# RWKV-6 attention feeding a squared-ReLU MLP: the order of the opening written anew

## The chip, the cores and the metric

The kernel runs on one core of one Trainium2 chip. The metric is device time in microseconds (us), the median of a few runs; lower is better. A core has five instruction queues that run beside each other and meet only at semaphores: PE (matrix products), DVE (vector engine), ACT (scalar engine), POOL (GpSimd) and SP, which here issues every DMA. Each engine takes its instructions strictly in program order, so an instruction that waits holds up all that stands behind it on the same engine.

## The reference

```python
for t in range(S):                       # r, k, v, w: (4, 8, 768, 48); u: (8, 48)
    cur = np.einsum('bhd,bhe->bhde', u[None] * kt, vt)
    y[:, :, t] = np.einsum('bhd,bhde->bhe', rt, state + cur)
    state = wt[:, :, :, None] * state + np.einsum('bhd,bhe->bhde', kt, vt)
...
h = x @ w_in                             # x: y as (3072, 384); w_in (384, 2048)
r = np.maximum(h, 0.0)
return ((r * r) @ w_out)                 # w_out (2048, 384)
```

A linear attention with a per-channel decay `w` and a bonus `u` for the current token, then a two-layer MLP (the names of the code call it MoE) on all 3072 tokens.

## The kernel before

**Tiles.** The 768 tokens of each of 4 batches are cut into 3 blocks of 256, so there are 12 steps, 0 to 11. In a step a partition holds two neighbouring tokens, and 64 partitions form a chunk. For each step the attention part makes a 256 x 384 block `y`; the MLP part multiplies it with `w_in` (8 groups of 256 columns) and `w_out` (4 groups of 512 rows for each half of the tokens).

**An order written by hand.** The text `ORDER` is the whole program. Each word names an operation, its step and further indices, after a colon the PSUM bank that it writes, after `=` the engine (A is ACT, V is DVE, G is POOL). The loop at the end of the kernel reads the words and calls one Python function for each; each engine's instruction order is the order of its words in the text. There is no planner.

**The words of a step s**, with the line by which the profile knows them:

- `ld.s.w/r/k/v` load 384 KB each (L201); `ld.0.u` loads the 1.5 KB of `u` into one partition (L229); `ld.g.i` and `ld.g.o` load 768 KB of `w_in` and `w_out` (L209, L214), and `cast.i.g`, `cast.o.g` turn them to fp16 (L221). All loads go through SP's one queue.
- `ub_` spreads `u` over the partitions by a product (L234), `uc_` copies it out of PSUM (L238).
- `ww_` multiplies neighbouring decays (L288), `lw_` takes the logarithm (L292), `cum_` makes prefix sums by products (L332 to L336), `exp_` and `ac_` take exponentials (L349, L356).
- `rw_` and `kw_` scale r and k by w (L300, L304); `rd_.s.0` and `rd_.s.1` apply the decays to r and k (L370); `tr_` transposes them on PE (L379) and `rkt_` copies the transposes to SBUF (L384).
- `p_` makes the r times k products (L404), two for a step, `pm_` masks them (L412 where they lie in two single banks, L415 in a double bank).
- `v_` casts v (L296); `su_` makes the state update (L426), `ts_` adds the old state (L434, L436), `sn_` decays the sum on POOL (L440).
- `ku_`, `qp_` on POOL, `q_` on DVE and `vq_` on POOL make the bonus term (L307, L312, L315, L318).
- `y_`, `yc_`, `yq_` add the three parts of y in one double bank (L450), `ysb_` copies it out (L488), `yt_` transposes it (L496), `xt_` copies that (L500).
- `m1_.s.g` are the six products of group g with `w_in` (L513); groups 2c and 2c+1 need `cast.i.c`. `rl_.s.g` applies ReLU (L520 on ACT, L522 on DVE), `sq_` squares (L528), `m2_.s.c.q` multiplies with `w_out` (L536), `os_` and `store` write out.
- `warm_.n.i` are n products of zeros of 512 columns into bank i (L618); their result is not used.

PSUM holds two double banks `att` (0 and 1) and four single banks `one` (0 to 3): a word that writes a bank waits until the last reader of its former contents is done.

The call that turns a word into instructions:

```python
for word in ORDER.split():
    ...
    operations[name](*args)
```

Of the kernel before, what the change touches and what calls it, by code (L numbers as in the profile page):

```python
# [14 lines left out]


ORDER = """
ld.0.w warm_.10.1 ld.1.w ld.0.u ld.0.r ld.0.k ld.1.k ww_.0=V lw_.0 ld.1.r cum_.0:1 ww_.1=V ub_:1 lw_.1 exp_.0 ld.0.v
rw_.0=G ac_.0 warm_.1.3 uc_=A cum_.1:0 ld.0.i kw_.0=V warm_.4.3 ku_.0 ac_.1 rd_.0.0 exp_.1 ld.1.v rd_.0.1 tr_.0.0:0
rkt_.0.0=A kw_.1=V ld.1.i tr_.0.1:1 rw_.1=G rd_.1.1 warm_.4.2 ld.2.i rkt_.0.1=A ld.3.i qp_.0 warm_.1.0 rd_.1.0 v_.0=A  # L20
ld.2.w p_.0.0:n pm_.0.0 su_.0:1 tr_.1.1:2 ts_.0.0=A q_.0 p_.0.1:0 rkt_.1.1=A sn_.0.0 warm_.4.0 pm_.0.1 ld.2.k
cast.i.0=A vq_.0 tr_.1.0:3 rkt_.1.0=V y_.0:0 v_.1=A ku_.1 ts_.0.1=V yc_.0 yq_.0 ld.2.r p_.1.1:n ysb_.0=A p_.1.0:1
pm_.1.1 cast.i.1=A yt_.0:3 sn_.0.1 su_.1:0 xt_.0=V qp_.1 ts_.1.0=V m1_.0.1:3 cast.i.2=A pm_.1.0 m1_.0.3:2 m1_.0.0:0
rl_.0.1=A sn_.1.0 q_.1 ld.2.v cast.i.3=A m1_.0.2:1 rl_.0.3=V m1_.0.4:3 vq_.1 ld.0.o ts_.1.1=V rl_.0.2=A y_.1:1
rl_.0.0=V yc_.1 ld.3.k ww_.2=G yq_.1 m1_.0.5:2 ysb_.1=V ku_.2 m1_.0.6:0 lw_.2 rl_.0.4=V rl_.0.5=A yt_.1:1 sq_.0.0=A
cum_.2:1 ld.1.o xt_.1=V m1_.0.7:3 ld.3.w kw_.2=G rl_.0.6=A m1_.1.1:1 ld.2.o exp_.2 sn_.1.1 m1_.1.4:2 rl_.1.1=V
rl_.0.7=A m1_.1.0:0 rw_.2=G sq_.0.3=A rl_.1.4=V m1_.1.5:1 rl_.1.0=V qp_.2 m1_.1.7:2 rd_.2.0 rl_.1.5=A m1_.1.6:0 ld.3.r
rl_.1.7=A rd_.2.1 tr_.2.0:3 cast.o.0=G rl_.1.6=A m1_.1.2:1 ld.3.o rkt_.2.0=V v_.2=A tr_.2.1:2 rl_.1.2=A m1_.1.3:0
ku_.3 rkt_.2.1=V ac_.2 sq_.1.0=A su_.2:0 q_.2 m2_.0.0.0:1 ld.4.w m2_.0.1.0:3 ts_.2.0=V sq_.0.1=A cast.o.1=G rl_.1.3=V
ld.3.v p_.2.0:1 p_.2.1:0 ww_.3=V sq_.1.1=A m2_.1.1.0:0 vq_.2 m2_.1.0.0:2 pm_.2.1 lw_.3 sq_.1.2=A m2_.0.0.1 pm_.2.0  # L30
m2_.1.1.1 sn_.2.0 sq_.1.3=A m2_.1.0.1 cast.o.2=A m2_.0.1.1 ld.4.k qp_.3 cum_.3:0 y_.2:1 sq_.0.2=A yc_.2 yq_.2 ld.4.r
q_.3 m2_.1.1.2 cast.o.3=A m2_.1.0.2 rw_.3=V ld.5.w ww_.4=G m2_.0.0.2 ysb_.2=V ac_.3 exp_.3 m2_.0.0.3 kw_.3=G ld.4.v
m2_.1.1.3 rd_.3.0 os_.0.0=A lw_.4 v_.3=G m2_.1.0.3 ld.5.r rd_.3.1 os_.1.1=A yt_.2:1 kw_.4=G cum_.4:1 os_.1.0=V xt_.2=A
tr_.3.0:0 ac_.4 su_.3:0 exp_.4 tr_.3.1:2 ld.5.v ts_.3.0=V rw_.4=G m2_.0.1.2 rkt_.3.0=V rkt_.3.1=A m1_.2.0:1 sn_.3.0
ld.6.w rd_.4.0 m2_.0.1.3 ww_.5=G ts_.3.1=V m1_.2.6:2 ld.5.k os_.0.1=A rd_.4.1 v_.4=G m1_.2.3:0 ld.7.w ku_.4 p_.3.1:1
rl_.2.3=A p_.3.0:0 pm_.3.1 m1_.2.1:3 lw_.5 rl_.2.0=A store.0.0 m1_.2.2:0 rl_.2.1=A dtr_.4.1 pm_.3.0 vq_.3 m1_.2.5:1
sq_.2.0=A su_.4:1 rl_.2.6=V rl_.2.5=A y_.3:0 qp_.4 rl_.2.2=V yc_.3 yq_.3 m1_.2.7:3 ysb_.3=A dtr_.4.0 m1_.2.4:1
sq_.2.1=A rl_.2.7=V sn_.3.1 cum_.5:0 v_.5=G yt_.3:2 ts_.4.0=V ac_.5 m2_.2.0.0:0 rl_.2.4=V xt_.3=A kw_.5=G m2_.2.0.1
q_.4 sq_.2.2=A m2_.2.1.0:2 sn_.4.0 rw_.5=V exp_.5 m2_.2.1.1 ku_.5 m2_.2.1.2 sq_.2.3=A rd_.5.0 m1_.3.7:1 rd_.5.1
dtr_.5.0 m1_.3.1:3 qp_.5 ts_.4.1=V m2_.2.1.3 rl_.3.1=A rl_.3.7=V dtr_.5.1 p_.4.1:0 p_.4.0:1 os_.2.1=V m1_.3.3:1  # L40
pm_.4.0 vq_.4 store.1.1 m2_.2.0.2 ld.6.r rl_.3.3=A pm_.4.1 m1_.3.2:2 ld.6.k sn_.4.1 m1_.3.0:3 ld.7.r rl_.3.2=A ww_.6=G
ld.7.k sq_.3.1=A su_.5:1 y_.4:0 ts_.5.0=V ww_.7=G yc_.4 q_.5 yq_.4 store.1.0 p_.5.0:1 ysb_.4=A m1_.3.5:2 ld.6.v
rl_.3.0=V lw_.7 m2_.2.0.3 pm_.5.0 yt_.4:1 os_.2.0=A m1_.3.4:3 ld.8.w xt_.4=V lw_.6 ku_.6 rl_.3.5=V p_.5.1:1 rl_.3.4=A
cum_.7:0 pm_.5.1 ld.8.r m1_.3.6:0 exp_.7 vq_.5 m1_.4.3:1 sq_.3.0=A rw_.7=V ld.7.v cum_.6:1 m1_.4.1:3 rl_.4.3=A kw_.7=G
m1_.4.0:2 rl_.4.1=A store.2.1 m1_.4.5:1 rl_.3.6=A rl_.4.0=V sn_.5.0 exp_.6 m2_.3.1.0:3 rd_.7.0 kw_.6=G sq_.3.2=A
m2_.3.0.0:0 rd_.7.1 m2_.3.0.1 rw_.6=G rl_.4.5=A m2_.3.1.1 sq_.3.3=A ww_.8=G rd_.6.0 m2_.3.0.2 ac_.7 m1_.4.4:1 qp_.6
rd_.6.1 dtr_.6.0 m2_.3.0.3 ac_.6 m1_.4.2:2 v_.6=A dtr_.6.1 ku_.7 q_.6 v_.7=A su_.6:1 y_.5:0 ld.11.w os_.3.0=V yc_.5
ld.9.w rl_.4.4=V vq_.6 yq_.5 ld.8.k m2_.3.1.2 rl_.4.2=V ysb_.5=A m2_.3.1.3 rw_.8=V ts_.6.0=A store.3.0 yt_.5:1 sn_.6.0
ld.8.v os_.3.1=A m1_.4.7:0 xt_.5=A qp_.7 m1_.4.6:3 ts_.6.1=V sq_.4.2=A m1_.5.7:2 rl_.4.6=A p_.6.1:1 rl_.5.7=V
store.0.1 p_.6.0:0 rl_.4.7=A sn_.6.1 m1_.5.0:1 pm_.6.1 lw_.8 m1_.5.1:3 sq_.4.0=A ld.9.k ww_.9=G pm_.6.0 m1_.5.5:0  # L50
rl_.5.1=A m1_.5.4:2 dtr_.7.0 sq_.4.3=A rl_.5.0=V y_.6:1 sq_.4.1=V rl_.5.5=A su_.7:0 yc_.6 rl_.5.4=A kw_.8=V yq_.6 q_.7
m2_.4.0.0:3 ysb_.6=A m1_.5.6:2 v_.8=A ts_.7.0=V dyt_.6 vq_.7 cum_.8:1 rl_.5.6=A m2_.4.1.0:0 ni_.8=V sq_.5.0=A dtr_.7.1
m2_.4.0.1 tw_.1=V sn_.7.0 m2_.4.0.2 ac_.8 exp_.8 store.3.1 m2_.4.0.3 ww_.11=V ld.9.r lw_.9 m1_.5.3:1 ku_.8 os_.4.0=A
ld.10.w rd_.8.1 m2_.4.1.1 sq_.5.2=A ld.9.v m2_.4.1.2 ts_.7.1=V rl_.5.3=A tw_.3=V m1_.5.2:3 dtr_.8.1 qp_.8 m1_.6.3:2
# [621 lines left out]
```

## Time and profile before

| | |
|---|---|
| runs of the kernel, us | 179.25, 179.38, 216.63; median 179.38 |
| the profiled execution | 178.85 us, of which 177.0 from its first to its last instruction |
| PE busy | 169.8 us, 96% of the span |
| DVE, ACT, POOL busy | 144.5, 136.9, 129.6 us |
| mean granted TensorE clock | 0.998 |
| bytes moved | 35.63 MB |

The profiled execution lies 0.53 us below the median. Times inside a profile count from the start of its span. A row of the timeline gives start, duration, engine, line, operation, output<-input with shapes, how many instructions were merged, and in square brackets how long the engine had been idle before and what ended that. `SPq` rows are issues of DMAs on SP's queue.

### The profile page before, as it was taken

The numbers are of one execution on the slowest core, as the hardware profiler recorded it, in microseconds if no ns is written. First come the engines' busy times: TensorE is split into PE (matmuls) and PEld (weight loads), VectorE is DVE, ScalarE is ACT, GpSimd is POOL, SyncE is SP. The second block draws the span as 40 slices with busy tenths as digits, with TensorE's granted clock in tenths as the row PEclk, the third lists the DMA queues.
The fourth block names the chain that finished last, engine by engine and source line by source line (L and its number), as shares of the span: only waits on it lengthen the run. The fifth ranks groups of instructions, "written<-read, shape, count | busy, mean of one in ns | idle before, by whom it ended". The sixth has DMA issues, their size and how long they took to land.

```text
span 177.0 us, 5877 instructions
## 1 busy us (share of the span) xinstructions
PE 169.8 (96%) x2458; PEld 135.5 (77%) x2458; DVE 144.5 (82%) x228; ACT 136.9 (77%) x225; POOL 129.6 (73%) x117
## 2 busy tenths in 40 slices
PE   7978899999999999999999999999999999999992
PEld 2355789756777687767867889888888888999992
DVE  6499967956787889768989999899999999559960
ACT  5779798998868756987998898999898855893301
POOL 6389999996699994989759709935996871282760
PEclk9999999999999999999999999999999999999999
DMA  5999999999999299989999979969969100410223
GB/s 156 325 357 390 354 231 368 355 351 249 299 254 204 47 219 323 275 194 211 311 137 209 280 63 242 211 95 278 198 152 163 45 3 4 133 48 0 87 95 133
DMA packets 78811, 35.63 MB, mean 201 GB/s; under 512 B 72129, under 2 KB 77250, under 8 KB 78786
## 3 DMA queue, kind: packets, MB, share of 16 engines
q1 hardware_dynamic: 78786, 35.27, 78.8%
q8 instruction: 19, 0.31, 0.7%
q14 instruction: 6, 0.05, 0.1%
HBM read 25.17 MB, written 4.72 MB: 169 GB/s over the span
## 4 chain that ended last, share of the span: by engine, by line
PE 73%; DVE 9%; DMA 7%; SPq 6%; issue 2%; POOL 1%; ACT 1%; ACTq 0%; DVEq 0%; POOLq 0%
PE one L513 29%; PE one L590 15%; PE one L536 15%; PE att L450 6%; DMA w_st_b<-in_moe_w_in_dram 5%; SPq L201 3%; DVE pmT_b L415 3%; PE att L404 3%; DMA r_b<-in_r_dram 2%; PE att L426 2%; DVE w_st_b L568 2%; SPq L209 1%; PE one L379 1%; DVE rdec_buf L370 1%; DVE q_b L315 1%
## 5 line engine op out<-in xcount | busy, mean ns | idle before, releaser
L513 PE MATMUL one<-xT_b,wi_sb 128*128 128x256 bf16 x576 | 70.8, 273 | 0.7 <-ACT gt_b L520 0.3
L513 PEld LDWEIGHTS <-wi_sb 128*128 128x128 f16 x576 | 54.9, 98 | 9.6 <-issue 1.5
L520 ACT ACTIVATE gt_b<-one 128x512 f16<-128x512 f32 x65 | 37.8, 596 | 12.1 <-PE one L513 11.2
L528 ACT ACTIVATE gt_b<-gt_b 128x1024 bf16<-128x1024 f16 x44 | 45.8, 1054 | 0.6 <-DVE gt_b L522 0.2
L536 PE MATMUL one<-wo_sb,gt_b 128*128 128x384 f16 x160 | 28.7, 326 | 0.0
L415 DVE TENSOR_TENSOR pmT_b<-att,mask 128x1024 bf16<-128x1024 f32 x22 | 26.2, 1214 | 1.3 <-PE att L404 1.3
L522 DVE TENSOR_SCALAR gt_b<-one 128x512 f16<-128x512 f32 x31 | 20.9, 685 | 5.4 <-PE one L513 4.4
L307 POOL TENSOR_TENSOR ku_b<-k_b,u_bc 128x768 f32<-128x768 f32 x12 | 22.4, 1869 | 3.0 <-DMA k_b<-in_k_dram 2.3
L440 POOL TENSOR_TENSOR S_b<-t_b,ac_buf 128x384 bf16<-128x384 f32 x20 | 18.1, 906 | 8.9 <-DVE t_b L436 4.5
L590 PEld LDWEIGHTS <-gt_b 128*128 128x128 bf16 x280 | 23.4, 98 | 0.6 <-issue 0.2
L312 POOL TENSOR_TENSOR ku_b<-ku_b,r_b 128x768 f32<-128x768 f32 x12 | 22.4, 1863 | 0.6 <-DMA r_b<-in_r_dram 0.4
L536 PEld LDWEIGHTS <-gt_b 128*128 128x128 bf16 x160 | 15.2, 98 | 9.2 <-issue 0.2
L318 POOL TENSOR_TENSOR vq_b<-v_b,q_b 128x768 bf16<-128x768 f32 x12 | 18.5, 1539 | 4.1 <-PE att L450 3.0
L590 PE MATMUL one<-wo_sb,gt_b 128*128 128x192 f16 x168 | 17.0, 246 | 0.0
L315 DVE TENSOR_REDUCE q_b<-ku_b 128x16 f32<-128x768 f32 x12 | 11.3, 945 | 3.7 <-POOL ku_b L312 3.7
L370 DVE TENSOR_TENSOR rdec_buf<-r_b,att 128x768 bf16<-128x768 f32 x12 | 11.4, 948 | 2.3 <-ACT att L349 1.8
L595 ACT ACTIVATE w_st_b<-one 128x192 f32<-128x192 f32 x13 | 4.3, 330 | 10.9 <-PE one L590 10.9
L300 POOL TENSOR_TENSOR r_b<-r_b,w_b 128x384 f32<-128x384 f32 x8 | 8.0, 1001 | 5.1 <-DMA r_b<-in_r_dram 5.1
L370 DVE TENSOR_TENSOR rdec_buf<-k_b,att 128x768 bf16<-128x768 f32 x12 | 11.4, 946 | 0.1
L568 POOL TENSOR_TENSOR gt_b<-gt_b 128x512 bf16<-128x512 bf16 x7 | 8.1, 1154 | 4.5 <-DVE w_st_b L568 4.0
L590 PE MATMUL one<-w_st_b,gt_b 128*128 128x192 f16 x112 | 11.2, 246 | 0.0
L488 ACT CAST y_sb_b<-att 128x768 bf16<-128x768 f32 x10 | 8.0, 799 | 3.8 <-PE att L450 3.6
(101 smaller groups left out, 276.8 us busy)
## 6 DMA issues: line engine op xcount, KB each, us to landing
...
rkT_b<-rdec_buf SPq DMA_TRANSPOSE x16, 3.5
```

The source lines that it names most:

```text
L307: nc.gpsimd.tensor_mul(buf("ku", s)[:], buf("k", s)[:, :, 1:3, :], u_bc[:, :, None, :].to_broadcast([C, H, 2, D]))
L312: nc.gpsimd.tensor_mul(ku[:], ku[:], buf("r", s)[:, :, 0:2, :])
L318: nc.gpsimd.tensor_mul(buf("vq", s)[:].rearrange("p j h d -> p h j d"), buf("v", s)[:], buf("q", s)[:, :, :, None].to_broadcast([C, H, 2, D]))
L370: nc.vector.tensor_mul(rdec[:, i, :, heads, 0:D], x.rearrange("p h j d -> p j h d"), decay[:, None, :, :].to_broadcast([C, 2, n, D]))
L415: nc.vector.tensor_mul(pmT, ps_p[:].rearrange("p e (a x) -> p (e a) x", a=2), mk.to_broadcast([C, 4, 2 * C]))
L440: nc.gpsimd.tensor_mul(buf("S", s + c, 1 - c)[:], buf("t", s, c)[:].rearrange("p (a e d) -> p a e d", a=HP, e=2), tiles["a_c", s][:, :, c, ...
L513: nc.tensor.matmul(ps1[:, j, :], wi_sb[:, n // 4, kk, n % 4 * 128:(n % 4 + 1) * 128], xT[:, :, kk, :], start=(kk == 0), stop=(kk == KT - 1))
L520: nc.scalar.activation(rl, m1, AF.Relu, scale=RS)
L522: nc.vector.tensor_scalar(out=rl, in0=m1, scalar1=RS, scalar2=0.0, op0=ALU.mult, op1=ALU.max)
L528: nc.scalar.activation(gt, rl, AF.Square)
L536: nc.tensor.matmul(m2, gt[:, n, c * C:(c + 1) * C], wo_sb[:, n, :], start=(n == 0), stop=(n == NT - 1))
L590: nc.tensor.matmul(where_to, gt[:, n, :], wo[:, n, :], start=(n == 0 and i in (1, 2, 5)), stop=(n == NT // 2 - 1), skip_group_check=True)
```

## The change

Only the text `ORDER` changes, and only up to the first products with `w_out` of step 0; from `m2_.0.1.0` on both texts have the same words in the same order. The operations are the same but for the warm products: 24 in six words before, 23 in four words after.

```diff
-ld.0.w warm_.10.1 ld.1.w ld.0.u ld.0.r ld.0.k ld.1.k ww_.0=V lw_.0 ld.1.r cum_.0:1 ww_.1=V ub_:1 lw_.1 exp_.0 ld.0.v
-rw_.0=G ac_.0 warm_.1.3 uc_=A cum_.1:0 ld.0.i kw_.0=V warm_.4.3 ku_.0 ac_.1 rd_.0.0 exp_.1 ld.1.v rd_.0.1 tr_.0.0:0
-rkt_.0.0=A kw_.1=V ld.1.i tr_.0.1:1 rw_.1=G rd_.1.1 warm_.4.2 ld.2.i rkt_.0.1=A ld.3.i qp_.0 warm_.1.0 rd_.1.0 v_.0=A
-ld.2.w p_.0.0:n pm_.0.0 su_.0:1 tr_.1.1:2 ts_.0.0=A q_.0 p_.0.1:0 rkt_.1.1=A sn_.0.0 warm_.4.0 pm_.0.1 ld.2.k
-cast.i.0=A vq_.0 tr_.1.0:3 rkt_.1.0=V y_.0:0 v_.1=A ku_.1 ts_.0.1=V yc_.0 yq_.0 ld.2.r p_.1.1:n ysb_.0=A p_.1.0:1
-pm_.1.1 cast.i.1=A yt_.0:3 sn_.0.1 su_.1:0 xt_.0=V qp_.1 ts_.1.0=V m1_.0.1:3 cast.i.2=A pm_.1.0 m1_.0.3:2 m1_.0.0:0
-rl_.0.1=A sn_.1.0 q_.1 ld.2.v cast.i.3=A m1_.0.2:1 rl_.0.3=V m1_.0.4:3 vq_.1 ld.0.o ts_.1.1=V rl_.0.2=A y_.1:1
...
+ld.0.u warm_.10.0 ld.0.w ld.1.w ld.0.r ld.0.k ld.1.k ww_.0=V lw_.0 ld.1.r cum_.0:1 ww_.1=V warm_.1.2 exp_.0 ub_:3
+ld.0.v rw_.0=V lw_.1 rd_.0.0 cum_.1:0 uc_=A ld.0.i kw_.0=V tr_.0.0:0 exp_.1 ku_.0 rd_.0.1 ld.1.v ac_.1 rkt_.0.0=V
+ac_.0 tr_.0.1:2 warm_.6.3 kw_.1=V ld.1.i rkt_.0.1=A rw_.1=G rd_.1.1 ld.2.i ld.3.i p_.0.0:m v_.0=A qp_.0 rd_.1.0
+tr_.1.1:0 ld.2.w rkt_.1.1=A su_.0:1 pm_.0.0 tr_.1.0:1 ts_.0.0=A p_.0.1:0 rkt_.1.0=A q_.0 sn_.0.0 warm_.6.3 cast.i.0=A
+ld.2.k pm_.0.1 vq_.0 p_.1.1:n ts_.0.1=V y_.0:0 v_.1=A pm_.1.1 ku_.1 yc_.0 ld.2.r yq_.0 p_.1.0:1 ysb_.0=A pm_.1.0
+cast.i.1=A yt_.0:3 qp_.1 su_.1:0 xt_.0=V y_.1:1 cast.i.2=A m1_.0.3:2 sn_.0.1 m1_.0.1:1 q_.1 rl_.0.3=A m1_.0.2:0 ld.2.v
+rl_.0.1=V cast.i.3=A vq_.1 m1_.0.4:3 ts_.1.0=V m1_.0.0:2 rl_.0.2=V ld.0.o rl_.0.4=A sn_.1.0 m1_.0.5:1 ww_.2=V ld.3.k
+yq_.1 kw_.2=G yc_.1 ts_.1.1=V lw_.2 m1_.0.6:3 rl_.0.0=V ysb_.1=A cum_.2:0 rl_.0.6=V sq_.0.0=A yt_.1:2 ld.1.o m1_.0.7:0
...
```

Sorted by engine, the words of the new opening stand in these orders:

- SP: `ld.0.u` comes first, then all other loads in the order that they had before.
- PE: `warm_.10 cum_.0 warm_.1 ub_ cum_.1 tr_.0.0 tr_.0.1 warm_.6 p_.0.0 tr_.1.1 su_.0 tr_.1.0 p_.0.1 warm_.6 p_.1.1 y_.0 yc_.0 yq_.0 p_.1.0 yt_.0 su_.1 y_.1 m1_.0.3 m1_.0.1 m1_.0.2 m1_.0.4 m1_.0.0 m1_.0.5 yq_.1 yc_.1 m1_.0.6 cum_.2 yt_.1 m1_.0.7`, then the groups of step 1 with `tr_.2` and `su_.2` among them.
- ACT: `lw_.0 exp_.0 lw_.1 uc_ exp_.1 ac_.1 ac_.0 rkt_.0.1 v_.0 rkt_.1.1 ts_.0.0 rkt_.1.0 cast.i.0 v_.1 ysb_.0 cast.i.1 cast.i.2 rl_.0.3 cast.i.3 rl_.0.4 lw_.2 ysb_.1`.
- DVE: `ww_.0 ww_.1 rw_.0 rd_.0.0 kw_.0 rd_.0.1 rkt_.0.0 kw_.1 rd_.1.1 rd_.1.0 pm_.0.0 q_.0 pm_.0.1 ts_.0.1 pm_.1.1 pm_.1.0 xt_.0 q_.1 rl_.0.1 ts_.1.0 rl_.0.2 ww_.2 ts_.1.1 rl_.0.0 rl_.0.6 xt_.1`.
- POOL: `ku_.0 rw_.1 qp_.0 sn_.0.0 vq_.0 ku_.1 qp_.1 sn_.0.1 vq_.1 sn_.1.0 kw_.2 rw_.2 sn_.1.1 ku_.2 qp_.2 cast.o.0`.

Other engines than before have `rw_.0` and `ww_.2` (POOL before, DVE now), `rkt_.0.0` (ACT, now DVE), `rkt_.1.0` and `ysb_.1` (DVE, now ACT), and ten `rl_` of steps 0 and 1. Several PSUM banks change with the order.

More of the change, by code (lines that the diff above doesn't have):

```diff
@@ L23 @@
-pm_.1.1 cast.i.1=A yt_.0:3 sn_.0.1 su_.1:0 xt_.0=V qp_.1 ts_.1.0=V m1_.0.1:3 cast.i.2=A pm_.1.0 m1_.0.3:2 m1_.0.0:0
-rl_.0.1=A sn_.1.0 q_.1 ld.2.v cast.i.3=A m1_.0.2:1 rl_.0.3=V m1_.0.4:3 vq_.1 ld.0.o ts_.1.1=V rl_.0.2=A y_.1:1
-rl_.0.0=V yc_.1 ld.3.k ww_.2=G yq_.1 m1_.0.5:2 ysb_.1=V ku_.2 m1_.0.6:0 lw_.2 rl_.0.4=V rl_.0.5=A yt_.1:1 sq_.0.0=A
-cum_.2:1 ld.1.o xt_.1=V m1_.0.7:3 ld.3.w kw_.2=G rl_.0.6=A m1_.1.1:1 ld.2.o exp_.2 sn_.1.1 m1_.1.4:2 rl_.1.1=V
-rl_.0.7=A m1_.1.0:0 rw_.2=G sq_.0.3=A rl_.1.4=V m1_.1.5:1 rl_.1.0=V qp_.2 m1_.1.7:2 rd_.2.0 rl_.1.5=A m1_.1.6:0 ld.3.r
@@ L28 @@
[L28 to L51, printed above, removed]
+ld.0.u warm_.10.0 ld.0.w ld.1.w ld.0.r ld.0.k ld.1.k ww_.0=V lw_.0 ld.1.r cum_.0:1 ww_.1=V warm_.1.2 exp_.0 ub_:3
@@ new lines @@
+rl_.0.1=V cast.i.3=A vq_.1 m1_.0.4:3 ts_.1.0=V m1_.0.0:2 rl_.0.2=V ld.0.o rl_.0.4=A sn_.1.0 m1_.0.5:1 ww_.2=V ld.3.k
+yq_.1 kw_.2=G yc_.1 ts_.1.1=V lw_.2 m1_.0.6:3 rl_.0.0=V ysb_.1=A cum_.2:0 rl_.0.6=V sq_.0.0=A yt_.1:2 ld.1.o m1_.0.7:0
+rw_.2=G xt_.1=V exp_.2 ld.3.w m1_.1.4:2 rl_.0.7=V sn_.1.1 rl_.0.5=A rd_.2.1 m1_.1.2:3 rl_.1.4=A ku_.2 m1_.1.0:0 ld.2.o
+v_.2=A rd_.2.0 m1_.1.1:2 rl_.1.0=A rl_.1.2=V m1_.1.6:1 ac_.2 qp_.2 rl_.1.1=V tr_.2.1:3 ld.3.r rl_.1.6=A su_.2:1
+rkt_.2.1=V sq_.0.3=A m1_.1.5:0 ld.3.o cast.o.0=G tr_.2.0:1 sq_.0.1=A rl_.1.5=V m1_.1.7:2 rkt_.2.0=V m1_.1.3:0
@@ new lines @@
+sq_.1.0=A ku_.3 ts_.2.0=V m2_.0.0.0:1 ld.4.w q_.2 rl_.1.7=A m2_.0.1.0:3 cast.o.1=G rl_.1.3=V ld.3.v p_.2.0:1 p_.2.1:0
+ww_.3=V sq_.1.1=A m2_.1.1.0:0 vq_.2 m2_.1.0.0:2 pm_.2.1 lw_.3 sq_.1.2=A m2_.0.0.1 pm_.2.0 m2_.1.1.1 sn_.2.0 sq_.1.3=A
+m2_.1.0.1 cast.o.2=A m2_.0.1.1 ld.4.k qp_.3 cum_.3:0 y_.2:1 sq_.0.2=A yc_.2 yq_.2 ld.4.r q_.3 m2_.1.1.2 cast.o.3=A
+m2_.1.0.2 rw_.3=V ld.5.w ww_.4=G m2_.0.0.2 ysb_.2=V ac_.3 exp_.3 m2_.0.0.3 kw_.3=G ld.4.v m2_.1.1.3 rd_.3.0 os_.0.0=A
+lw_.4 v_.3=G m2_.1.0.3 ld.5.r rd_.3.1 os_.1.1=A yt_.2:1 kw_.4=G cum_.4:1 os_.1.0=V xt_.2=A tr_.3.0:0 ac_.4 su_.3:0
@@ new lines @@
+exp_.4 tr_.3.1:2 ld.5.v ts_.3.0=V rw_.4=G m2_.0.1.2 rkt_.3.0=V rkt_.3.1=A m1_.2.0:1 sn_.3.0 ld.6.w rd_.4.0 m2_.0.1.3
+ww_.5=G ts_.3.1=V m1_.2.6:2 ld.5.k os_.0.1=A rd_.4.1 v_.4=G m1_.2.3:0 ld.7.w ku_.4 p_.3.1:1 rl_.2.3=A p_.3.0:0 pm_.3.1
+m1_.2.1:3 lw_.5 rl_.2.0=A store.0.0 m1_.2.2:0 rl_.2.1=A dtr_.4.1 pm_.3.0 vq_.3 m1_.2.5:1 sq_.2.0=A su_.4:1 rl_.2.6=V
+rl_.2.5=A y_.3:0 qp_.4 rl_.2.2=V yc_.3 yq_.3 m1_.2.7:3 ysb_.3=A dtr_.4.0 m1_.2.4:1 sq_.2.1=A rl_.2.7=V sn_.3.1
+cum_.5:0 v_.5=G yt_.3:2 ts_.4.0=V ac_.5 m2_.2.0.0:0 rl_.2.4=V xt_.3=A kw_.5=G m2_.2.0.1 q_.4 sq_.2.2=A m2_.2.1.0:2
@@ new lines @@
+sn_.4.0 rw_.5=V exp_.5 m2_.2.1.1 ku_.5 m2_.2.1.2 sq_.2.3=A rd_.5.0 m1_.3.7:1 rd_.5.1 dtr_.5.0 m1_.3.1:3 qp_.5
+ts_.4.1=V m2_.2.1.3 rl_.3.1=A rl_.3.7=V dtr_.5.1 p_.4.1:0 p_.4.0:1 os_.2.1=V m1_.3.3:1 pm_.4.0 vq_.4 store.1.1
+m2_.2.0.2 ld.6.r rl_.3.3=A pm_.4.1 m1_.3.2:2 ld.6.k sn_.4.1 m1_.3.0:3 ld.7.r rl_.3.2=A ww_.6=G ld.7.k sq_.3.1=A
+su_.5:1 y_.4:0 ts_.5.0=V ww_.7=G yc_.4 q_.5 yq_.4 store.1.0 p_.5.0:1 ysb_.4=A m1_.3.5:2 ld.6.v rl_.3.0=V lw_.7
+m2_.2.0.3 pm_.5.0 yt_.4:1 os_.2.0=A m1_.3.4:3 ld.8.w xt_.4=V lw_.6 ku_.6 rl_.3.5=V p_.5.1:1 rl_.3.4=A cum_.7:0 pm_.5.1
@@ new lines @@
+ld.8.r m1_.3.6:0 exp_.7 vq_.5 m1_.4.3:1 sq_.3.0=A rw_.7=V ld.7.v cum_.6:1 m1_.4.1:3 rl_.4.3=A kw_.7=G m1_.4.0:2
+rl_.4.1=A store.2.1 m1_.4.5:1 rl_.3.6=A rl_.4.0=V sn_.5.0 exp_.6 m2_.3.1.0:3 rd_.7.0 kw_.6=G sq_.3.2=A m2_.3.0.0:0
+rd_.7.1 m2_.3.0.1 rw_.6=G rl_.4.5=A m2_.3.1.1 sq_.3.3=A ww_.8=G rd_.6.0 m2_.3.0.2 ac_.7 m1_.4.4:1 qp_.6 rd_.6.1
+dtr_.6.0 m2_.3.0.3 ac_.6 m1_.4.2:2 v_.6=A dtr_.6.1 ku_.7 q_.6 v_.7=A su_.6:1 y_.5:0 ld.11.w os_.3.0=V yc_.5 ld.9.w
+rl_.4.4=V vq_.6 yq_.5 ld.8.k m2_.3.1.2 rl_.4.2=V ysb_.5=A m2_.3.1.3 rw_.8=V ts_.6.0=A store.3.0 yt_.5:1 sn_.6.0 ld.8.v
@@ L52 @@
+os_.3.1=A m1_.4.7:0 xt_.5=A qp_.7 m1_.4.6:3 ts_.6.1=V sq_.4.2=A m1_.5.7:2 rl_.4.6=A p_.6.1:1 rl_.5.7=V store.0.1
+p_.6.0:0 rl_.4.7=A sn_.6.1 m1_.5.0:1 pm_.6.1 lw_.8 m1_.5.1:3 sq_.4.0=A ld.9.k ww_.9=G pm_.6.0 m1_.5.5:0 rl_.5.1=A
+m1_.5.4:2 dtr_.7.0 sq_.4.3=A rl_.5.0=V y_.6:1 sq_.4.1=V rl_.5.5=A su_.7:0 yc_.6 rl_.5.4=A kw_.8=V yq_.6 q_.7
 m2_.4.0.0:3 ysb_.6=A m1_.5.6:2 v_.8=A ts_.7.0=V dyt_.6 vq_.7 cum_.8:1 rl_.5.6=A m2_.4.1.0:0 ni_.8=V sq_.5.0=A dtr_.7.1
```

## The prediction

> **What bounds the kernel now.** I read the chain of waits first. It names what released each step back from the end.
>
> ```profile
> 0.74 0.46 SPq L201
> ...
> 10.57 9.38 DMA w_st_b<-in_moe_w_in_dram
> 20.00 1.36 issue
> 21.36 0.60 ACT gt_b L520
> 21.96 0.04 issue
> 22.00 0.82 PE one L513 x6
> 22.81 1.25 PE att L450 x52
> 24.07 1.42 PE one L513 x12
> ...
> 26.24 4.58 PE one L513 x42
> ```
>
> The columns are start, duration, what. Up to 20.0 us the chain runs through SP's queue and the third `w_in` load; from 22.00 on it lies on PE, with no gap until 97.6. Then the busy time by stretch (PE comes first behind the length):
>
> ```profile
> 8.00:10.00 2.00, 1.13 (x12) 0.47 (x10) 2.00 (x4) 1.27 (x5) 1.81 (x1) 1.00 1.17 325
> 22.00:33.40 11.40, 11.40 (x160) 9.71 (x159) 8.52 (x13) 10.49 (x17) 11.03 (x9) 1.00 1.04 311
> 33.40:97.60 64.20, 64.20 (x915) 47.09 (x914) 51.65 (x67) 53.16 (x85) 54.80 (x44) 1.00 0.98 239
> ```
>
> PE is full from 22 us. The DMA engines are full from the first load on (share 1.17, 325 GB/s), so loads land in a gapless train: w.0 at 4.0, w.1 5.2, r.0 6.5, k.0 7.65, k.1 8.8, r.1 10.2, v.0 11.2, `w_in` group 2 at 19.98, group 3 at 22.0, w.2 at 23.15 (issue time plus time to landing). What the change is worth is therefore how much sooner or later PE begins `m2_.0.0.0` (33.47 in the chain): the work behind it is the same in the same order. The timeline gives the prices:
>
> ```profile
> 0.74 1.08 SPq L201 DMA_DIRECT2D w_b<-in_w_dram  x2
> 1.87 0.80 SPq L229 DMA_DIRECT2D u_row<-in_u_dram  x1
> 2.71 0.39 SPq L201 DMA_DIRECT2D r_b<-in_r_dram  x1
> ...
> 6.54 1.00 POOL L300 TENSOR_TENSOR r_b<-r_b,w_b 128x384 f32<-128x384 f32 x1 [2.72 <-DMA r_b<-in_r_dram]
> ...
> 8.13 0.95 DVE L370 TENSOR_TENSOR rdec_buf<-r_b,att 128x768 bf16<-128x768 f32 x1
> ...
> 11.77 0.42 PE L404 MATMUL one<-rkT_b 64*64 64x128 bf16 x16
> ...
> 18.89 2.78 PE L513 MATMUL one<-xT_b,wi_sb 128*128 128x256 bf16 x24 [0.20 <-DVE xT_b L500]
> ...
> 19.98 1.47 ACT L221 CAST wi_sb<-w_st_b 128x1536 f16<-128x1536 f32 x1 [0.93 <-DMA w_st_b<-in_moe_w_in_dram]
> ```
>
> **u first.** w.0 and w.1 are issued later by one issue of u; r.0 and all behind keep their place in SP's queue. But the train is gapless from w.0, so a later w.0 moves every landing. The price is between 0.43 (the shortest load issue, 0.39, and 0.04 between issues) and 0.85 (u's own 0.80 and 0.05). I take 0.51: an issue into an empty queue, as u's will be, cost 0.46 for w.0, while u's 0.80 was paid behind two loads. Nothing is won in exchange, as u's 1.5 KB were there long before `ub_` ran at 5.99. Everything below is first reckoned with the old landings; the shift d = 0.51 is added at the end, since each stretch starts from a landing.
>
> [...]
>
> **Up to p_.0.0.** Before, `rd_.0.0` began at 8.13 behind `kw_.0`, which waited for k.0 until 7.65. Now `exp_.0` runs ahead of `lw_.1` (6.1 to 6.9 instead of 6.29 to 7.08), `rw_.0` takes 0.55 on DVE (L300 rows there: 0.55 and 0.72) from r.0's landing, to 7.06, and `rd_.0.0` runs 7.06 to 8.0. `kw_.0` to 8.5, `rd_.0.1` to 9.4, eight transposes to 9.95 (0.5 to 0.6 as in L379). `rkt_.0.0` (0.69 on DVE) is done at 10.05, `rkt_.0.1` (0.96 on ACT) at 11.0. Six warm products at 0.22 stand in between (five took 1.24), to 11.27. So `p_.0.0` starts at 11.3: 0.45 sooner.
>
> **Up to the first MoE product.** This lead is spent. ACT: `v_.0` from v.0's landing, 11.2 to 12.05; `rkt_.1.1` 12.3 to 13.25, now ahead of `ts_.0.0`, to 13.73 (13.53 before); `rkt_.1.0`, which was on DVE, to 14.7; `cast.i.0` 1.48, to 16.15; `v_.1` 0.83, to 16.95; `ysb_.0` 0.80, to 17.75 (17.68 before). On DVE `pm_.1.0` (1.22) now stands ahead of `xt_.0`: `pm_.0.0` to 13.6, `q_.0` 14.5, `pm_.0.1` 15.7, `ts_.0.1` 16.2, `pm_.1.1` 17.4, `pm_.1.0` 18.6, `xt_.0` 19.15 (18.84 before). `y_.1` (0.5) runs on PE at 18.65 while `xt_.0` is waited for, so it costs nothing there. If that cover were gone it would cost its 0.5. `cast.i.1` ends at 19.2. First product 19.2, that is 0.3 later than before.
>
> **Up to m2_.0.0.0.** Three groups of six at 0.655 end at 21.15, and PE idles until `cast.i.2` (19.98 + 1.47) lets `m1_.0.4` go at 21.5. Before, the four groups that needed no new cast ended at 21.67, and `m1_.0.4` waited until 22.00 for `rl_.0.1`, which stood behind the same cast on ACT. This wait is gone: group 4 takes a bank that `xt_.0` has freed. Next late is `rl_.0.3`, behind the cast at 22.05, and `m1_.0.0` in its bank: it fits behind group 4 (22.15 to 22.8). `m1_.0.5` to 23.45, `yq_.1` and `yc_.1` to 24.1 (52 products with y took 1.25, 32 of them `y_.1`). ACT: `rl_.0.3`, `cast.i.3` to 23.5, `rl_.0.4` to 24.1; `m1_.0.6` waits for it and runs 24.15 to 24.8 (25.48 before). Here PE leads by 0.7. `cum_.2` to 25.2; `yt_.1` waits for `ysb_.1` behind `lw_.2` on ACT (25.42), so `m1_.0.7` starts at 25.8 against 26.24: the lead is 0.44. Further on, PE waits 0.05 for `rl_.1.4` at 28.4 and about 0.05 for `rl_.1.2` at 29.75; `su_.2` needs `v_.2`, done at 29.2. `m2_.0.0.0` starts at 33.1 against 33.47: lead 0.37.
>
> **Sum.** -0.37 + 0.51 = +0.14 us, with the bounds of u's price +0.06 to +0.48. One warm product less (0.22) lies beside waits and gives nothing. POOL loses `rw_.0` and `ww_.2`, 2.0 us of its 129.6, but its `cast.o.0` ends at 32.5 instead of 32.0, since `ku_.2` now stands behind `sn_.1.1`. Cover: `m2_.0.0.0` needs it at 33.1, and POOL then waits for r.3 until 38.1 in any case. The later stages shift with PE.
>
> The profiled execution would go from 178.85 to 178.99. It lies 0.53 below the median of the runs, so I forecast 179.5 against 179.38.
>
> **Rivals.**
>
> 1. *The train does not move*: u's issue runs beside the start-up of the transfers, as the first bytes of w.0 move about 1 us after its issue began, and full rate came at 2.6. Then only the lead of 0.37 counts: 179.0. Against it: w.0's landing, 3.3 us after its issue, is the start of all the rest, and nothing shows that a load of 1.5 KB shortens it. Chance 0.27.
>
> 2. *PE loses its clock in the opening* (slower). The first ten warm products took 4.45 us, 0.43 each, the four at 7.49 only 1.02, 0.25 each: PE starts at half pace and becomes fast about 5.4. Before, PE was busy 3.5 of the 4.4 us from 5.6 to 10; now, with one warm product there in place of five, I estimate 2.6. If that is too little, `tr_.0.1` and six warm products run at half pace: 0.4 + 1.3 = 1.7 us later for `p_.0.0`, and ACT has no slack to take it up. With the forecast's own +0.14 that makes 181.2. It decides if PE is at half pace past 9.5. Against it: no gap grows past 1.4 us, and the trace shows full pace after PE's idle 0.62 before 9.13. Chance 0.10. If half pace lasted until 19, PE's work on this path up to there (the L379, L404, L426, L450 and L496 rows and twelve warm products, some 4 us) would double: chance 0.02 more.
> [...]
>
> 3. *DVE stalls on w.2* (slower). `ww_.2` waited on POOL for w.2 until 23.19 with only POOL's words behind it. On DVE, `ts_.1.1`, `rl_.0.0`, `rl_.0.6` and `xt_.1` stand behind it, and PE waits for these from 25.85 on. From the landing they need 0.56 + 0.54 + 0.68 + 0.69 = 2.5, so each 0.1 us that w.2 lands after 23.4 (beyond the shift) costs as much. Its load took 10.5 us from issue to landing, the neighbours' 9.4 to 10.9; a landing 1.2 later costs 0.9: 180.4. Chance 0.08.
>
> That the change does not do what it says: `y_.1` does come ahead of the products, but not sooner in time than its mask allows; this is in the sum.
>
> **How the numbers follow.** Forecast 0.50 (179.2 to 179.9), rival 1 0.27, rival 2 0.12, rival 3 0.08, the rest 0.03. The range 178.5 to 181.1 holds the forecast, rival 1 with 0.5 below it, and rival 3; it stops short of rival 2. A change of 2%, 3.6 us, is about what a measurement of this kernel can tell from none. Only rival 2 in its long form goes past it, and the rest in part: faster 0.02, within 0.95, slower 0.03.
>
> **What would show it.** u's issue at 0.74, about 0.46 long, `ww_.0` starting at 4.5; `p_.0.0` at 11.8, the first L513 row at 19.7, `m1_.0.4` behind a cast that starts at 20.5, `m2_.0.0.0` at 33.6, and PE full from there. Wrong if w.0 lands as before (rival 1), if L618 or L379 rows after 8 us take half pace (rival 2), or if DVE idles for w.2 (rival 3); and if the gain or loss comes behind 34 us, where I have it unchanged.

## The result, and the profile after

The changed kernel takes 182.39 us (median of four runs, 182.19 to 182.64) against 179.37: a ratio of 1.0172, interval 1.015 to 1.0193. It is slower by 1.7%, where +0.1 us was forecast. The profiled execution took 182.19 us, 3.34 more than that of before; from its first to its last instruction it is 180.1 us against 177.0. The ratios compare the runs that lie within 1.5% of the fastest of their kernel and the medians are of all runs, so a ratio is not the quotient of two medians.

Nearly all of the loss arises in the opening. I matched each matrix product of the two traces by its line and number and took the difference of the start times:

| product | before, us | after, later by |
|---|---|---|
| first with `w_out` (L536, step 0) | 33.41 | 3.07 |
| 73rd of L536 | 57.99 | 3.06 |
| last of L536 | 97.91 | 3.05 |
| 121st of L590 | 130.42 | 3.06 |
| last of L590 | 173.58 | 3.06 |

So the loss is complete when the two texts become equal (from `cast.o.1` on, two words behind `m2_.0.1.0`), and nothing is given back or added in the 140 us behind. The chain of waits after (start, duration, what) shows where it lies:

```profile
1.14 3.47 DMA w_b<-in_w_dram
7.73 0.94 DVE rdec_buf L370
8.67 1.94 DVE k_b L304
10.64 0.97 DVE rdec_buf L370
11.65 1.03 PE one L379 x8
12.68 2.56 PE one L618 x6
...
22.83 4.04 PE one L513 x36
```

SP's queue no longer leads it. In its place stand a k product on DVE (`kw_.0`) that lasts 1.94, eight transposes that take 1.03, and six warm products that take 2.56. The timeline of DVE, then that of POOL:

```profile
8.59 2.02 DVE L304 TENSOR_TENSOR k_b<-k_b,w_b 128x384 f32<-128x384 f32 x1
10.64 0.95 DVE L370 TENSOR_TENSOR rdec_buf<-k_b,att 128x768 bf16<-128x768 f32 x1
11.51 0.68 DVE L384 COPY rkT_b<-one 128x1024 bf16<-128x1024 bf16 x1
12.11 1.85 DVE L304 TENSOR_TENSOR k_b<-k_b,w_b 128x384 f32<-128x384 f32 x1
```

```profile
8.38 1.80 POOL L307 TENSOR_TENSOR ku_b<-k_b,u_bc 128x768 f32<-128x768 f32 x1 [4.56 <-DMA k_b<-in_k_dram]
10.79 0.99 POOL L300 TENSOR_TENSOR r_b<-r_b,w_b 128x384 f32<-128x384 f32 x1 [0.60 <-DMA r_b<-in_r_dram]
11.74 1.81 POOL L312 TENSOR_TENSOR ku_b<-ku_b,r_b 128x768 f32<-128x768 f32 x1
```

Read the two side by side: `kw_.0` ends at 10.61, 0.4 after `ku_.0` ends on POOL (10.18), and `kw_.1` at 13.96, 0.4 behind `qp_.0` (13.55). Before, they took 0.56 and 0.55: `kw_.0` ran at 7.65, ahead of `ku_.0` (8.11), and `kw_.1` at 9.86, just as `ku_.0` ended (9.92):

```profile
7.65 0.56 DVE L304 TENSOR_TENSOR k_b<-k_b,w_b 128x384 f32<-128x384 f32 x1 [1.89 <-DMA k_b<-in_k_dram]
...
8.11 1.81 POOL L307 TENSOR_TENSOR ku_b<-k_b,u_bc 128x768 f32<-128x768 f32 x1 [0.57 <-ACT u_bc L238]
...
9.86 0.55 DVE L304 TENSOR_TENSOR k_b<-k_b,w_b 128x384 f32<-128x384 f32 x1
```

I read the 2.02 and 1.85 as the 0.56 and 0.55 of work and a wait for POOL, which the profile shows as part of the instruction. It is no wait for data: `kw_` writes a part of k that `ku_` does not read, and in the text of the change `ku_.0` stands behind `kw_.0`. Nor is it a slower pace: whenever such a row begins, it ends the same 0.4 behind POOL. The 17 traces of this document hold 266 rows of this product on DVE (L288, L300, L304); 99 of them last more than 0.62 us (4 of 15 in the trace of before, 7 of 17 in that of after), and each of these ends 0.40 to 0.43 behind a POOL row that began earlier. The trace of before has such rows further on:

```profile
70.63 1.48 POOL L318 TENSOR_TENSOR vq_b<-v_b,q_b 128x768 bf16<-128x768 f32 x1
71.22 1.31 DVE L300 TENSOR_TENSOR r_b<-r_b,w_b 128x384 f32<-128x384 f32 x1
```

In the other order POOL waits: in two of the runs below (`b3` and `d3`) `kw_.0` began just ahead of `ku_.0` and kept its 0.56, and `ku_.0` took 2.12 instead of 1.81.

So in these rows the one that began first kept its time: POOL's two took their usual 1.80 and 1.81 in the change, and DVE ended 0.4 behind them. `rd_.0.1`, which reads one operand from PSUM, kept its 0.95 (10.64) beside POOL's `rw_.1` (10.79, 0.99). The section on the cores says that the queues meet only at semaphores; these two meet elsewhere too, and what they share is not shown.

The second finding is PE's clock. Busy times by stretch (length, PE first; granted clock third from the end):

```profile
5.01:8.43 3.42, 2.63 (x17) 0.82 (x15) 2.00 (x4) 2.13 (x5) 0.05 (x1) 1.00 1.17 323
8.43:11.84 3.41, 1.23 (x11) 0.97 (x12) 3.38 (x4) 1.32 (x5) 2.81 (x3) 0.50 1.14 337
11.84:15.25 3.41, 3.41 (x18) 1.47 (x20) 3.31 (x4) 1.89 (x3) 1.71 (x1) 0.50 1.09 365
```

The clock rose at 5.01, fell to half at 8.43 and rose again at 15.25. Before, it rose at 5.53 and stayed: there the ten warm products from 1.19 on took 4.45 and the four at 7.49 took 1.02. The mean granted clock was 0.978 to 0.981 in all eight runs of the changed kernel (these four and four on another chip, `c0_after`), so the fall is not that of one trace.

### The profile page after: what moved, and what is told of

Its sections match the earlier page's. It is cut to its first block, busy times and chain, and to the rows that moved or that the text cites. A ratio compares the mean times of both kernels' runs of the same rounds, so it can differ in the third digit from the quotient of the medians.

```text
span 180.1 us, 5870 instructions
## 1 busy us (share of the span) xinstructions
PE 171.6 (95%) x2457; PEld 136.0 (75%) x2457; DVE 149.2 (83%) x231; ACT 135.7 (75%) x224; POOL 127.8 (71%) x115
## 4 chain that ended last, share of the span: by engine, by line
PE 77%; DVE 11%; DMA 4%; ACT 3%; issue 2%; POOL 1%; SPq 0%; ACTq 0%; DVEq 0%; POOLq 0%
PE one L513 30%; PE one L590 14%; PE one L536 14%; PE att L450 6%; DVE pmT_b L415 3%; PE att L404 3%; PE att L426 2%; DMA r_b<-in_r_dram 2%; DVE rdec_buf L370 2%; PE one L379 2%; DMA w_b<-in_w_dram 2%; DVE w_st_b L568 2%; PE one L618 1%; DVE k_b L304 1%; PE one L496 1%
## 5 line engine op out<-in xcount | busy, mean ns | idle before, releaser
L520 ACT ACTIVATE gt_b<-one 128x512 f16<-128x512 f32 x63 | 36.5, 597 | 11.9 <-PE one L513 11.3
L536 PE MATMUL one<-wo_sb,gt_b 128*128 128x384 f16 x160 | 28.7, 326 | 0.0
L522 DVE TENSOR_SCALAR gt_b<-one 128x512 f16<-128x512 f32 x33 | 22.3, 685 | 5.8 <-PE one L513 4.6
L590 PEld LDWEIGHTS <-gt_b 128*128 128x128 bf16 x280 | 23.4, 98 | 0.6 <-issue 0.2
L536 PEld LDWEIGHTS <-gt_b 128*128 128x128 bf16 x160 | 15.2, 98 | 9.2 <-ACT gt_b L528 0.2
L590 PE MATMUL one<-wo_sb,gt_b 128*128 128x192 f16 x168 | 17.0, 246 | 0.0
L488 ACT CAST y_sb_b<-att 128x768 bf16<-128x768 f32 x11 | 8.8, 799 | 3.7 <-PE att L450 3.7
L590 PE MATMUL one<-w_st_b,gt_b 128*128 128x192 f16 x112 | 11.2, 246 | 0.0
L349 ACT ACTIVATE att<-att 128x768 f32<-128x768 f32 x12 | 9.6, 799 | 2.0 <-PE att L336 1.3
```

Source lines behind the costliest of these rows:

```text
L520: nc.scalar.activation(rl, m1, AF.Relu, scale=RS)
L522: nc.vector.tensor_scalar(out=rl, in0=m1, scalar1=RS, scalar2=0.0, op0=ALU.mult, op1=ALU.max)
L536: nc.tensor.matmul(m2, gt[:, n, c * C:(c + 1) * C], wo_sb[:, n, :], start=(n == 0), stop=(n == NT - 1))
L590: nc.tensor.matmul(where_to, gt[:, n, :], wo[:, n, :], start=(n == 0 and i in (1, 2, 5)), stop=(n == NT // 2 - 1), skip_group_check=True)
```

## The experiments

Two theories are set apart. Theory L: the loss is the wait of DVE for POOL. Theory C: the loss is the fall of PE's clock.

The experiments ran on four chips; that of the first pair is not on record. Times in them scatter more: the kernel before took 178.7 to 182.2, with medians from 179.2 to 179.9, and most traces lose 0.2 to 1.6 more behind 75 us, where the texts are equal. So next to the ratio I give how much later than 33.41 the first product with `w_out` starts; this contains the opening alone. In the one other trace of the unchanged kernel it was 0.45 (below), so differences under 0.5 between single traces mean little.

| run | median, us | ratio to before (interval) | later by, us | half clock, us |
|---|---|---|---|---|
| the change | 182.39 | 1.0172 (1.015 to 1.0193) | 3.07 | 8.4 to 15.3 |
| e1_u_third | 181.95 | 1.0049 (1.0001 to 1.0098) | 3.30 | 9.4 to 16.2 |
| e2_kw_pool | 181.19 | 1.0054 (1.0022 to 1.0086) | 2.33 | 8.3 to 15.1 |
| e3_warm | 183.10 | 1.0126 (1.0066 to 1.0187) | 2.83 | none |
| e4_kw_warm | 181.42 | 1.0070 (1.0039 to 1.0101) | 1.23 | none |
| b1_u_first | 180.35 | 1.0010 (0.997 to 1.0051) | 0.47 | none |
| b2_kw_behind_rd | 181.69 | 1.0075 (1.0039 to 1.0111) | 2.76 | 13.0 to 16.4 |
| b3_four_warm_less | 180.15 | 1.0012 (0.9972 to 1.0051) | 1.45 | 11.0 to 14.4 |
| e5_kw_warm_u | 181.21 | 1.0067 (1.0026 to 1.0108) | 0.84 | none |
| c0_before | 179.34 | 0.9997 (0.9963 to 1.003) | 0.45 | none |
| c0_after | 182.60 | 1.0174 (1.0121 to 1.0228) | 3.07 | 7.6 to 14.4 |
| c1_mixed | 181.13 | 1.0090 (1.0061 to 1.012) | 1.04 | none |
| c2_no_overlap | 183.22 | 1.0212 (1.0164 to 1.026) | 3.23 | 20.3 to 23.7 |
| d1_cast_behind | 179.30 | 0.9989 (0.9974 to 1.0004) | 0.00 | none |
| d2_wait_clock_kept | 182.48 | 1.0160 (1.012 to 1.02) | 2.58 | none |
| d3_y_ahead | 179.10 | 0.9983 (0.9958 to 1.0007) | 0.10 | none |

**Undoing parts of the change.** `e1_u_third`: `ld.0.u` back behind `ld.1.w`.

> The changed kernel with the load of u put back to third place in SP's queue. If u's place costs what its issue costs, w.0 lands at 4.0 instead of 4.6, all of the opening starts 0.6 us sooner, and the time falls by 0.6, to 181.8. If the loss lies elsewhere alone (DVE held up by POOL, or PE at half pace, neither of which this touches), the time stays at 182.2 to 182.4 though w.0 lands sooner.

w.0 landed sooner, but the first product with `w_out` did not start sooner. The clock's steps lay otherwise in this execution: it rose at 5.96, fell at 9.37 and came back only at 16.20, 0.95 later than in the changed kernel. The runs of this kernel spread from 179.4 to 182.7, and its clock with them: eleven have a mean granted clock of 0.980 to 0.991 and took 180.5 or more; one kept the clock (1.00) and took 179.41, no more than the kernel before. That run was not traced, and whether DVE waited in it is open. So this experiment says nothing clean about u.

`e2_kw_pool`:

```diff
-kw_.0=V
+kw_.0=G
...
-kw_.1=V
+kw_.1=G
```

> The changed kernel with kw_.0 and kw_.1 on POOL instead of DVE, so that they no longer run on DVE beside ku_.0 and qp_.0 on POOL, where they took 2.02 and 1.85 us instead of 0.56. Theory L (DVE's products of two SBUF tensors wait for the running POOL instruction, and that wait is the loss): kw takes 1.0 each on POOL, the r decay of step 1 (L370) ends at 14.1 instead of 15.9, and the time falls by 1.3 to 1.8, to 180.6 to 181.1, though PE is still at half pace. Theory C (the loss is PE at half pace from 8.5 to 14.9): warm products and transposes still end at about 15, and the time falls by less than 0.5.

`e3_warm`:

```diff
-warm_.10.0
+warm_.11.0
...
 ub_:3
+warm_.1.2
...
 cum_.1:0
+warm_.2.1
...
 tr_.0.0:0
+warm_.8.1
```

> The changed kernel with PE kept busy from 1 to 11 us by twelve more warm products (one more in the first word, one behind the product that spreads u, two behind cum_.1, eight behind the transposes of r of step 0). Theory C: the granted clock stays at 1.00 between 8 and 15 us, the six warm products ahead of p_.0.0 take 1.3 instead of 2.8, and the time falls by 1.5 or more. Theory L: the clock stays as well, but kw_.0 and kw_.1 still take 2.0 and 1.85 on DVE, the decays of step 1 still end at 15.9, and the time falls by 0.6 at most.

`e4_kw_warm`: both edits.

> Both edits: kw_.0 and kw_.1 on POOL and twelve more warm products. If the waits of DVE and the half pace hide each other in part (each covers the other's time ahead of p_.0.0 and its mask), the two together give more than the sum of each alone: 2.2 to 2.8 less, 179.6 to 180.2, and u's 0.6 is what is left to the kernel before. If either theory holds alone, the better of the two single runs is met within 0.3.

Against the change, `kw` on POOL alone brought 0.74 us in the opening, less than theory L gave; the clock alone 0.24; both together 1.84, less than the 2.2 to 2.8 that I expected of them. Each of the first two is within or little above what single traces differ by; 1.84 is far above it. The median of `e3_warm` is even 0.7 above that of the change, as its trace loses 1.6 more behind 75 us. The two causes hide each other: with the clock kept, DVE's wait still ends the decays of step 1 at 15.86 and PE has nothing to do; with the wait gone, `p_.0.0` still stands behind warm products at half pace (2.77 for six). In `e4_kw_warm` the chain shows what the edit itself costs:

```profile
8.59 1.00 POOL k_b L304
...
11.31 1.00 POOL k_b L304
12.31 0.97 POOL r_b L300
...
14.18 1.28 DVE pmT_b L412 x2
15.46 0.86 DVE q_b L315
16.32 1.14 DVE pmT_b L415
```

POOL now carries 2 us of `kw` ahead of `rw_.1` and `qp_.0`, and the mask behind `q_.0` waits for these.

`e5_kw_warm_u`: all three undone.

> The changed kernel with all three undone: kw_.0 and kw_.1 on POOL, twelve more warm products, u in third place. If the three make up the loss, the first product with w_out starts 0.6 sooner than with the first two (34.1 against 34.64; 33.41 before), and the time is within 0.7 of the kernel before. If something of the loss is still unnamed, 1.2 or more remain.

The opening was 0.84 behind that of before; the kernel before itself was 0.45 behind on another chip. The time is 0.67% higher, not within 0.7 us: this trace loses 1.2 more behind 75 us, where the texts are equal. Of that I have no cause.

**One part of the change alone, in the kernel before.** `b1_u_first`: `ld.0.u` ahead of `ld.0.w`.

> The kernel before with the load of u in first place and nothing else changed. If u's place alone costs what w.0's later landing says (4.60 instead of 4.01), everything up to the first products with w_out starts 0.6 us later and the time rises by 0.6. If PE also loses its clock in the longer gap, the time rises by 1 to 2. If the loads' start does not bound the opening, it stays within 0.2.

`ww_.0` started at 4.62, `kw_.0` at 8.26 (7.65 before), and the opening was 0.47 later with the clock kept.

`b2_kw_behind_rd`:

```diff
-kw_.0=V
...
 rd_.0.0
+kw_.0=V
```

> The kernel before with kw_.0 moved behind rd_.0.0 on DVE, so that it would start at 8.5 while ku_.0 runs on POOL (8.1 to 9.9). Theory L: kw_.0 takes about 1.9 us instead of 0.56, rd_.0.1 starts at 10.4 instead of 9.0, kw_.1 then meets qp_.0 on POOL and takes as long again, and the time rises by 2 to 3, although every other word of the opening is that of before. Without such a wait: rd_.0.0 starts at 7.6 instead of 8.1 and the time falls by up to 0.3.

This one word brings 2.76 of the 3.07 us in the opening. The wait is there (1.84 for `kw_.0`, 2.13 for `kw_.1`), but PE idles behind it, and the clock fell from 13.0 to 16.4; the two were still mixed. So `d2_wait_clock_kept` adds `warm_.9.3` behind `tr_.0.0:0`:

> The kernel before with kw_.0 behind rd_.0.0 on DVE, as in the earlier run, and nine more warm products behind the transposes of r of step 0, so that the clock stays at 1.00. Theory L alone: kw_.0 and kw_.1 take 1.8 to 2.1 each, the decays of step 1 end at about 15.6 as they did there, and the first product with w_out starts 2.0 to 2.5 later than in the kernel before (33.4 to 33.9). If the wait needed the fall of the clock to cost anything, it starts less than 1 later.

Its timeline, DVE and then POOL:

```profile
7.76 0.95 DVE L370 TENSOR_TENSOR rdec_buf<-r_b,att 128x768 bf16<-128x768 f32 x1 [1.85 <-POOL r_b L300]
8.63 1.84 DVE L304 TENSOR_TENSOR k_b<-k_b,w_b 128x384 f32<-128x384 f32 x1
10.51 0.95 DVE L370 TENSOR_TENSOR rdec_buf<-k_b,att 128x768 bf16<-128x768 f32 x1
11.38 2.13 DVE L304 TENSOR_TENSOR k_b<-k_b,w_b 128x384 f32<-128x384 f32 x1
```

```profile
8.25 1.81 POOL L307 TENSOR_TENSOR ku_b<-k_b,u_bc 128x768 f32<-128x768 f32 x1 [0.57 <-ACT u_bc L238]
10.30 1.02 POOL L300 TENSOR_TENSOR r_b<-r_b,w_b 128x384 f32<-128x384 f32 x1 [0.25 <-DMA r_b<-in_r_dram]
11.29 1.80 POOL L312 TENSOR_TENSOR ku_b<-ku_b,r_b 128x768 f32<-128x768 f32 x1
```

With the clock at 1.00 throughout, the opening is 2.58 later. The nine warm products cost nothing there: they ended at 11.34, and `rd_.0.1`, which the next transposes need, at 11.46. In each pair POOL starts first, by 0.38 and 0.09, and DVE ends 0.4 behind POOL. The wait alone makes 2.6 us (0.45 of it may be the chip's). With the fall of the clock, `b2` was later by 0.18 more, which two traces can't tell from nothing.

`b3_four_warm_less`: `warm_.4.3` taken out.

> The kernel before without the four warm products behind cum_.1. Theory C: the granted clock falls to half at about 8.9, the transposes and the five warm products ahead of p_.0.0 take twice as long, p_.0.0 starts at about 13.1 instead of 11.8 and the time rises by 0.8 to 1.5. If the four do not matter, the clock stays at 1.00 and the time within 0.2.

The clock fell at 10.99, two steps after its rise at 4.17 and not at about 8.9, and the opening was 1.45 later; but k.0 also landed 0.66 later here (`kw_.0` at 8.31 with its 0.56), and the edit touches no load. If that delay passed on in full, about 0.8 is left for the clock. The median rose by 0.4, inside its interval: the price of the clock alone is seen in one trace and not resolved in time.

**The two kernels once more, and what is left of the change's idea.**

> The kernel before, unchanged, profiled on the chip of this call: what part of the shifts measured in the experiments is the chip's. If the opening is the same on every chip, the first product with w_out starts at 33.4 and the span is 177.0; if loads start later here, 33.6 to 34, with one more stop of PE behind 75 us, and the span is about 177.8.

> The changed kernel, unchanged, on the same chip. [...] The first product with w_out starts 2.5 to 3.3 later than in the kernel before on this chip, and the time is 1.5% above it.

On this chip the kernel before started the first product with `w_out` 0.45 later and the changed one at the very same 36.48, so here the change costs 2.63 in the opening; its `kw` took 2.14 and 1.85.

`c1_mixed` takes the words of before up to `v_.0`, then those of the change with `p_.0.0:m` ahead, and

```diff
-rkt_.1.0=A
...
 pm_.0.1
+rkt_.1.0=V
...
-pm_.1.0
...
 xt_.0=V
+pm_.1.0
...
-y_.1:1
...
 m1_.0.2:0
+y_.1:1
```

> The order of before up to v_.0, then the order of the change, with xt_.0 ahead of pm_.1.0 again, rkt_.1.0 on DVE as before, and y_.1 of step 1 behind three groups of products. No DVE product of two SBUF tensors meets a long POOL instruction in the opening, u is third, PE has the warm products of before. If the second half of the change is sound (22.8 to 36.6 in its own trace, 13.8 us from first product to first product with w_out, against 14.5 before), this starts the first product with w_out 0.4 sooner than the kernel before on this chip and ends 0.2 to 0.6 below it. If the second half is not, it ends at or above it.

It lost 1.0: the change's PE order has `p_.1.1` ahead of `y_.0`, and `p_.1.1` waited for `rkt_.1.0` until 16.31, and its first group needs `cast.i.1`, which ended at 20.1 (PE idle 0.42 for it).

`c2_no_overlap`: u third; `uc_` behind `rkt_.0.1`, `ku_.0` behind `rw_.1`, `kw_.1` ahead of `rkt_.0.0`, `ub_:1`, seven more warm products.

> The changed kernel's own order with nothing left of the three causes: u in third place, seven more warm products up to the transposes, and on POOL rw_.1 ahead of ku_.0, which now waits for a later copy of u, so that kw_.0 and kw_.1 (ahead of rkt_.0.0) run alone on DVE at 0.56 each. The prediction's own reckoning, with the landings of before, then holds: p_.0.0 at 11.3 to 11.7, the first product at 19.2, and the first product with w_out 0.2 to 0.4 sooner than in the kernel before on this chip. If it is more than 0.5 later, something else in the order costs time.

Up to there the reckoning of the prediction held: `kw_.0` 0.55 at 8.52, `kw_.1` 0.55 at 9.98, `p_.0.0` at 11.96. But the edit made a new wait: `ku_.0` ran only at 12.25, so `q_.0` waited 1.92 for `qp_.0`, and the mask behind it with it (`pm_.0.1` at 16.85 instead of 14.36 before). It shows that `ku_.0` has no room to be late, not what the rest of the order is worth.

`d1_cast_behind` moves `cast.i.2=A` behind `rl_.0.1=A` in the kernel before; `d3_y_ahead` moves `y_.1:1` ahead of `m1_.0.4:3` there.

> The kernel before with the word of cast.i.2 behind that of rl_.0.1 on ACT, and nothing else. PE's stop ahead of m1_.0.4 (0.33 in the profile of before, 0.59 in the run of before on the other chip) was a wait for rl_.0.1 behind this cast: rl_.0.1 now runs at 19.6 to 20.2, the cast to 21.7, and m1_.0.4 starts as soon as PE is free or the cast is done. The first product with w_out starts 0.2 to 0.5 sooner than in the kernel before, 0.1 to 0.3% of the time. If PE only waits for the next thing (cast.i.3, vq_.1), nothing is gained.

> The kernel before with y_.1 ahead of the fifth group m1_.0.4 on PE, and nothing else: y_.1 runs at 21.7 to 22.1 in PE's stop, m1_.0.4 behind it, and the first product with w_out starts 0.3 to 0.4 sooner than in the kernel before. If the mask of step 1 or rl_.0.1 is later than y_.1, it is the same as before.

`d3_y_ahead` takes PE's stop away, `d1_cast_behind` all but 0.09 of it. PE from the first group on, in `c0_before` (0.59 idle) and in `d3_y_ahead`:

```profile
19.08 2.78 PE L513 MATMUL one<-xT_b,wi_sb 128*128 128x256 bf16 x24 [0.20 <-DVE xT_b L500]
22.44 0.81 PE L513 MATMUL one<-xT_b,wi_sb 128*128 128x256 bf16 x6 [0.59 <-ACT gt_b L520]
```

```profile
19.36 2.79 PE L513 MATMUL one<-xT_b,wi_sb 128*128 128x256 bf16 x24 [0.20 <-DVE xT_b L500]
22.08 0.57 PE L450 MATMUL att<-v_bf_b,pmT_b 64*128 64x48 bf16 x32
22.59 0.83 PE L513 MATMUL one<-xT_b,wi_sb 128*128 128x256 bf16 x6
```

From the first product to the first with `w_out` it is 14.52 us in the profile of before (18.89 to 33.41), 14.14 in `d3_y_ahead`, 14.29 in `d1_cast_behind`. The medians are 0.34 and 0.14 us below those of the kernel before (0.9983 and 0.9989), and both intervals still hold 1. They are the best that came out. The change's own idea, y of step 1 into PE's stop, does remove the stop; whether either kernel beats the one before is not resolved.

## Why the prediction was wrong

**The step that failed** is "`kw_.0` to 8.5, `rd_.0.1` to 9.4", and with it the 0.55 of `kw_.1`, which the sum holds without naming it. I priced both by their rows of before, in which POOL had not begun or was just ending its instruction, and moved them to a place where POOL is in the middle of one. `kw_.0` ended at 10.61 and `kw_.1` at 13.96; the reckoning with the shift gave 9.0 and 11.1 (10.05 and 0.55 behind `rkt_.0.0`, plus 0.51). That `d2` gives 2.58 with nothing but this wait, the clock kept, shows that it suffices. The trace of before held the warning: the same product of 384 columns on DVE (L288, L300) took 0.55 in most rows but 1.18 at 92.54 and 1.31 at 71.22. I quoted 0.55 and 0.72 and did not ask what made the difference; the 0.72, at 58.08, also ends 0.4 behind a row of POOL.

**Rival 2** happened, and I gave it 0.12. Its argument against, that no gap grows past 1.4, was wrong twice: DVE's wait made a gap of 1.9 ahead of 11.65, and the clock had fallen before that, at the end of a stretch whose longest gap was 0.47. The six warm products ahead of `p_.0.0` took 2.77 where the sum has 1.32. Its price in time was also wrong, because I took it alone: of the 1.7 us, 0.24 came back when the clock was kept (`e3`), since the wait on DVE covered the rest. With the wait taken away first it was 1.10 (`e2` to `e4`).

**u first**: forecast 0.51, measured 0.61 (`ww_.0` at 4.62 with u first, 4.01 before): w.0's issue began 0.40 later, with u's issue itself 0.33, and w.0 landed 3.47 behind its issue instead of 3.25. Of this some is the trace's: w.0 landed at 4.50 to 4.62 in the six traces with u first and at 3.99 to 4.29 in the other eleven, and before's is the earliest of them. In the kernel before, u first alone gave 0.47 in the opening. Rival 1 fell: the train moved.

**The lead up to `p_.0.0`** (0.45) never came to be: it started at 15.17 instead of 11.8. In `c2`, where nothing overlaps, it started at 11.96, which the same working, with that run's w.0 (0.27 later than before), gives as 11.6.

**From the first product on** the forecast came out in size: 13.9 us from the first product to the first with `w_out`, measured 13.72 (22.76 to 36.48), 0.80 less than before. `y_.1` ran at 22.16, ahead of the products, as reckoned. This gain is in the result; without it the loss would be 3.9. The agreement is in part luck: the forecast has PE stop several times here, 0.35 of it for `cast.i.2`, and the trace has no stop at all, as PE came 3.9 later than before and the load behind that cast only 0.7 later (20.68 instead of 19.98).

**Rival 3** did not occur as such: w.2 had long landed when DVE came to `ww_.2`. It took 1.19 there beside `sn_.1.0` on POOL, the same wait once more. **That the later stages shift with PE** was right to 0.02 us.

My range ended at 181.1 and the result was 182.39, because the mechanism that is enough to make it, DVE's wait for POOL (2.58 in `d2`), was not among the rivals. What the wait and the clock each cost in the changed kernel stays open, since they cover each other; and with both and u undone, 0.8 is left (`e5`), part of it perhaps the chip's and part the price of `kw` on POOL.
